# Sending exp(scores) and u through HBM to transpose them on VectorE, with q and k fetched in one DMA each

## The chip, the core and the metric

The kernel runs on one core of a Trainium2 chip. The time is device microseconds of one launch, from the first to the last instruction and what lies around them; the median of three runs is given. Engines are called PE (TensorE, matmuls), DVE (VectorE), ACT (ScalarE), POOL (GpSimd) and SP (SyncE, which here only issues DMAs). Each engine works through its own list of instructions in order; semaphores make one wait for another.

## The reference

Attention within chunks of 64 tokens, 8 heads of 64 channels, feeds a low-rank mixer along the sequence and a two-layer channel network. Cut to what matters:

```python
# q, k, v: [B=8, H=8, S=576, D=64]
scores = scale * q_c @ k_c.T                    # per chunk of 64 tokens: 64x64
attn = exp(scores - scores.max()) ; attn /= attn.sum()
x = (attn @ v_c) -> [B, S, H*D = 512]
u = x + ((x^T @ U) @ V)^T                       # along the sequence, rank 32
out = u + relu(u @ w_ch1) @ w_ch2               # 512 -> 2048 -> 512
```

## The kernel before

Two batches make a *pair*: 1152 tokens, 9 tiles t of 128 tokens, 3 groups g of 3 tiles. Four pairs are worked off one after the other. fp32 products are formed from a high and a low part rounded to TensorE's fp32r type (three products for one), so u is held as uth and utl, the hidden layer as hh and hl.

The main work is 4 x 3 x 16 = 192 *blocks*: a block is one piece f of 128 hidden channels for one group. It has 12 h matmuls (L690, `hidden`), then hh by ACT (L698, relu) and hl by DVE (L703), then 9 o matmuls (L716, `project_out`). The o matmuls of block f stand behind the h matmuls of block f+1 on PE, so hh and hl have the length of 12 h matmuls and no more. All weights stay in SBUF once loaded in pair 0.

The side work of each tile has to be finished before its group's blocks, and is spread between the blocks of earlier ones:

- *Attention.* `load_qk` and `load_v` fetch q, k, v (qn, kn, vn). qT and kT: transposes. sc: 16 small matmuls (L482). mx and ex on DVE (L496, L500), exp on ACT (L504). Four PE transposes ps_eT (L452) and an ACT copy (L474) make eT. av: 16 small matmuls (L513), then row sums and the scaling on DVE (L525 to L532), which gives x.
- *Mixer.* `project_ops`: xh (ACT, L593), xl (DVE, L597), y matmuls over tiles (L604, L605). `mix_ops`: u matmul (L644), x + u on DVE (L650, written over x), four PE transposes ut (L656), then uth (ACT, L664) and utl (DVE, L669).

For q and k of all tiles but the first nine, DVE's 32x32 stream transpose (L460) is used, which turns each 32x32 square in place. A whole transpose needs the squares to be exchanged as well, and that is done by the layout of the load: the *halvings* (L382) copy q and k within HBM into buffers halfq and halfk in pieces of 32 channels (128 bytes), and L409 then fetches each tile by 8 DMAs of 64 KB, 32 partitions each, whose slowest loop runs over the 32 rows.

The order has two sources. Pair 0 is planned: each operation is an `Op` with its engine, a cost and buffers to take, and a list scheduler orders them together with the weight loads (table `WORK`) and the blocks (`STRETCHES`). `HALVES_FROM = 4` says from which block on halvings may go. From pair 0's last group on, the code is written in program order: `plan` gives a list of steps for each group (`attend`, `mixes`, `proj`), spread evenly over the 64 slots of the group (one slot ahead of each tile of a block), and each engine takes its instructions in this order where the data allow it. All later DMAs go on SP's one queue. Side work's buffers are 8 shared slots of 256 KB (`slot`); x has 10 buffers.

Of the kernel before, what the change touches and what calls it, by code (L numbers as in the profile page):

```python
# [21 lines left out]
def kernel(  # L22
# [11 lines left out]
    nc = tc.nc  # L34
# [87 lines left out]
    ROOM = {"bank": 8, "w": NF, "slot": NS, "x": NX, "y": 2, "ut": 2, "h": 2, "mx": 2, "sm": 2}  # L122
# [198 lines left out]
    def w_ops(f, after=None):  # L321
# [15 lines left out]
        for z in range(n):  # L337
            cols = slice(z * size, (z + 1) * size)

            def room(z=z):  # L340
                return wslot((size,), U32, f"wroom_{f}") if n == 1 else slot(U32, f"wroom_{f}_{z}")
# [13 lines left out]
            tag = "w" if n == 1 else "slot"  # L355
# [14 lines left out]

    loaded = {}
# [6 lines left out]
    hidden_last = [None]  # L378

    def halve(b, z, g):  # L380
        d = halves[b, z, g] = dram.tile([S, H * SQ], F32, name=f"half{'qk'[z]}_{b}_{g}")
        moved = nc.sync.dma_start(  # L382
            d.rearrange("s (h i) -> s h i", h=H),
            (q, k)[z][b, :, :, g * SQ : (g + 1) * SQ].rearrange("h s i -> s h i"),
        )
        sync = mybir.DependencyInfo(mybir.DependencyClass.Sync, mybir.DependencyReason.DATA)
        tc.add_manual_dep(moved.ins, hidden_last[0].ins.name, sync, reason="after this block")

    def halvings(pr):
        return [lambda b=b, z=z, g=g: halve(b, z, g) for b in (2 * pr, 2 * pr + 1) for z in range(2) for g in range(2)]  # L390

    def load_qk(pr, t):
# [5 lines left out]
        else:  # L398
            qn = slot(F32, "qn_" + n, (P, P // SQ, P))
            kn = slot(F32, "kn_" + n, (P, P // SQ, P))  # L400
            vn = slot(F32, "vn_" + n, (P, 2, HP, D1))
        nc.gpsimd.memset(vn[:, :, :, D:], 1.0)  # L402
        if not early(pr, t):
            for z, dst in enumerate((qn, kn)):
                for r, m, b, s0 in segments(pr, t):
                    for e in range(2):
                        for g in range(2):
                            x0 = (2 * e + g) * SQ
                            nc.sync.dma_start(  # L409
                                dst[x0 : x0 + SQ, r // SQ : (r + m) // SQ, :],  # L410
                                halves[b, z, g][s0 : s0 + m, e * P : (e + 1) * P].rearrange(
                                    "(a j) c -> j a c", j=SQ
                                ),
                            )
            loaded[pr, t] = qn, kn, vn
            return
# [5 lines left out]
    def heads(pr, t, e):  # L422
        return slice(e, None, 2) if early(pr, t) else slice(e * HP, (e + 1) * HP)
# [19 lines left out]

    def attention_ops(pr, t, *after):
        n = f"{pr}_{t}"
        st = {}
        mine = early(pr, t)

# [9 lines left out]
        def squares(z, name):  # L458
            dst = slot(F32, name + n, (P, HP, P))
            nc.vector.transpose(  # L460
                dst.rearrange("p h (a j) -> p h a j", j=SQ),
                loaded[pr, t][z].rearrange("p a (h i) -> p h a i", i=SQ),
            )
# [34 lines left out]
        def subtract(e):  # L498
            mx = st["mx"][:, e, :]
            nc.vector.tensor_sub(st["ex"][:, :, e, :], st["sc"][e], mx.unsqueeze(2).broadcast_to([P, HP, C]))  # L500

        def exp():
            exf = st["ex"].rearrange("p a b k -> p (a b k)")
            nc.scalar.activation(exf, exf, AF.Exp, scale=SCALE)  # L504

# [22 lines left out]
        def scaled(e):  # L528
# [428 lines left out]
```

## Time and profile before

| | |
|---|---|
| median of 3 runs | 988.29 us (985.99 to 989.6) |
| the profiled execution | 984.5 us |
| its span, first to last instruction | 982.7 us |
| mean granted TensorE clock | 0.99 |

The profile is of one execution. A row of a group has the instruction, its count after x, then the busy time in us and the mean ns of one, and then how long the engine stood idle just before them and which engine or DMA ended that. Rows of windows have, after the bounds and length, the busy us of PE, PEld (weight loads), DVE, ACT and POOL with instruction counts, the granted clock, the DMA engines' mean busy share and GB/s. Rows of a timeline have the start, the length, the engine and the instruction, and in brackets the idle time before it. Rows of DMAs have the queue, the count, the KB of each and the median us from issue to landing.

### The profile page before, as it was taken

The page shows a single profiled execution, that of the slowest core. Times are in us where ns is not written, and L with a number is a line of the kernel's source. Part 1 is how long each engine was busy: PE and PEld are TensorE (multiplying, and loading weights), DVE is VectorE, ACT ScalarE, POOL GpSimd, SP SyncE. Part 2 cuts the span into 40 slices and gives each one's busy share as a digit, 9 for nine tenths or more (in the row PEclk, how much of TensorE's full clock was granted, in tenths as well). Part 3 has the DMA queues.
Part 4 walks back from the last instruction along what each step waited for, and adds up shares of the span by engine and source line. Part 5 has one row for each costly group of instructions (what it writes and reads, how often), then busy time and mean ns, then how long its engine had stood idle before and what let it go on. Part 6 is the DMA issues. An engine that isn't in the chain of part 4 may idle for free.

```text
span 982.7 us, 16528 instructions
## 1 busy us (share of the span) xinstructions
PE 961.3 (98%) x6854; PEld 835.0 (85%) x6857; DVE 439.5 (45%) x867; ACT 227.5 (23%) x406; POOL 33.7 (3%) x89
## 2 busy tenths in 40 slices
PE   7899899999999999999999999999999999999998
PEld 4569799988888889888888888888888889999997
DVE  5789789874442534233443343333433333211211
ACT  4543333321321211111211221111212121111110
POOL 6500000000000000000000000000000000000000
PEclk8999999999999999999999999999999999999999
DMA  9945964146753121433332111111121000000000
GB/s 218 224 140 97 210 187 139 36 133 112 129 107 89 31 41 52 81 61 86 68 79 62 28 33 37 42 37 48 42 57 33 33 1 1 33 1 1 33 1 33
DMA packets 208123, 70.58 MB, mean 72 GB/s; under 512 B 164768, under 2 KB 200640, under 8 KB 208048
## 3 DMA queue, kind: packets, MB, share of 16 engines
q1 hardware_dynamic: 206528, 66.35, 29.9%
q0 software_dynamic: 1520, 3.17, 1.6%
q8 instruction: 54, 0.88, 0.4%
q14 instruction: 21, 0.17, 0.1%
HBM read 59.98 MB, written 23.67 MB: 85 GB/s over the span
## 4 chain that ended last, share of the span: by engine, by line
PE 91%; DMA 3%; DVE 3%; ACT 1%; SPq 1%; issue 1%; POOL 0%; DVEq 0%; ACTq 0%; POOLq 0%
PE h L690 41%; PE o L716 40%; PE sc L482 2%; PE av L513 2%; PE ut L656 2%; PE ps_eT L452 1%; DMA wraw<-in_moe_w_ch_dram 1%; PE u L644 1%; DMA qkv<-in_k_dram 1%; PE y L604 1%; PE y L605 1%; DMA uraw<-in_moe_U_dram 1%; DMA qkv<-in_v_dram 1%; PE y L611 1%; ACT qkT L474 0%
## 5 line engine op out<-in xcount | busy, mean ns | idle before, releaser
L690 PE MATMUL h<-uth,w 128*128 128x384 f32 x1536 | 424.8, 341 | 0.0
L716 PE MATMUL o<-w,hh 128*128 128x512 f32 x1152 | 359.2, 401 | 3.7 <-ACT hh L698 3.5
L690 PEld LDWEIGHTS h<-uth,w 128*128 128x128 f32 x1536 | 282.1, 188 | 8.2 <-issue 0.2
L703 DVE SCALAR_TENSOR_TENSOR hl<-h,hh 128x384 fp32r<-128x384 f32 x192 | 106.5, 555 | 361.3 <-ACT hh L698 361.1
L690 PE MATMUL h<-utl,w 128*128 128x384 f32 x768 | 260.0, 339 | 0.0
L716 PEld LDWEIGHTS o<-w,hh 128*128 128x128 f32 x1152 | 211.6, 189 | 42.2 <-ACT hh L698 5.6
L716 PE MATMUL o<-w,hl 128*128 128x512 f32 x576 | 217.7, 397 | 0.0
L698 ACT ACTIVATE hh<-h 128x384 fp32r<-128x384 f32 x192 | 94.2, 491 | 499.9 <-PE h L690 499.6
L690 PEld LDWEIGHTS h<-utl,w 128*128 128x128 f32 x768 | 144.8, 189 | 6.1 <-DVE utl L669 0.3
L716 PEld LDWEIGHTS o<-w,hl 128*128 128x128 f32 x576 | 108.7, 189 | 25.8 <-DVE hl L703 0.3
L504 ACT ACTIVATE ex<-ex 128x512 f32<-128x512 f32 x36 | 22.8, 633 | 97.0 <-DVE ex L500 94.0
L496 DVE TENSOR_REDUCE mx<-sc 128x4 f32<-128x256 f32 x72 | 27.9, 417 | 27.5 <-PE sc L482 27.4
L650 DVE TENSOR_TENSOR x<-u,x 128x512 f32<-128x512 f32 x36 | 24.3, 684 | 27.6 <-PE u L644 27.4
L460 DVE STREAM_TRANSPOSE qT<-qn 128x512 f32<-128x512 f32 x27 | 19.1, 708 | 31.8 <-PE y L604 15.6
L669 DVE TENSOR_TENSOR utl<-ut,uth 128x512 fp32r<-128x512 f32 x36 | 24.4, 687 | 19.8 <-ACT uth L664 19.8
L474 ACT COPY eT<-ps_eT 128x512 f32<-128x512 f32 x36 | 21.0, 587 | 42.6 <-PE ps_eT L452 19.8
L597 DVE TENSOR_TENSOR xl<-x,xh 128x512 fp32r<-128x512 f32 x30 | 20.5, 687 | 21.6 <-ACT xh L593 18.4
L500 DVE TENSOR_TENSOR ex<-sc,mx 128x256 f32<-128x256 f32 x72 | 28.0, 416 | 1.2 <-DVE mx L496 0.5
L664 ACT CAST uth<-ut 128x512 fp32r<-128x512 f32 x36 | 20.9, 587 | 32.2 <-PE ut L656 32.1
L532 DVE TENSOR_TENSOR x<-av,sm 128x256 f32<-128x256 f32 x72 | 27.1, 417 | 1.1
L402 POOL MEMSET vn<- 128x8 f32 x27 | 3.0, 112 | 685.1 <-PE y L605 205.3
L728 DVE TENSOR_TENSOR x<-o,x 128x512 f32<-128x512 f32 x36 | 23.1, 684 | 4.9 <-PE o L716 4.8
(84 smaller groups left out, 552.3 us busy)
## 6 DMA issues: line engine op xcount, KB each, us to landing
wraw<-in_moe_w_ch_dram SPq DMA_DIRECT2D x32, 512.0 KB, 7.1
out_dram<-x SPq DMA_DIRECT2D x36, 256.0 KB, 2.2
halfq<-in_q_dram SPq DMA_DIRECT2D x12, 576.0 KB, 6.3
halfk<-in_k_dram SPq DMA_DIRECT2D x12, 576.0 KB, 6.1
vn<-in_v_dram SPq DMA_DIRECT2D x108, 64.0 KB, 2.4
qn<-halfq SPq DMA_DIRECT2D x96, 64.0 KB, 2.0
kn<-halfk SPq DMA_DIRECT2D x96, 64.0 KB, 2.0
qkv<-in_v_dram POOLq DMA_DIRECT2D x36, 64.0 KB, 6.3
```

The lines of the kernel that those rows point to most:

```text
L474: nc.scalar.copy(dst.rearrange("p a b -> p (a b)"), st[name])
L496: nc.vector.reduce_max(mx, st["sc"][e], axis=AX.X)
L500: nc.vector.tensor_sub(st["ex"][:, :, e, :], st["sc"][e], mx.unsqueeze(2).broadcast_to([P, HP, C]))
L504: nc.scalar.activation(exf, exf, AF.Exp, scale=SCALE)
L532: nc.vector.tensor_mul(by_head[:, heads(pr, t, e), :], st["av"][e][:, :, 0:D], st["sm"][:, e].unsqueeze(2).broadcast_to([P, HP, D]),)
L650: nc.vector.tensor_add(x, st["u"], x)
L669: nc.vector.tensor_sub(ul[:, :, js], st["t"].rearrange("p (c t) -> p c t", c=NCC), uh[:, :, js])
L690: hidden_last[0] = nc.tensor.matmul(ps[:, :GN], lhsT=w[:, z, cc], rhs=u[:, cc, :], start=(n == 0), stop=(n == 3 * NCC - 1))
L698: nc.scalar.activation(hh, ps[:, :GN], AF.Relu)
L703: nc.vector.scalar_tensor_tensor(hl, ps[:, :GN], 0.0, hh, op0=ALU.max, op1=ALU.subtract)
L716: nc.tensor.matmul(acc[g, j], lhsT=h[:, js], rhs=w2[f][:, z], start=(first and i == 0), stop=(final and i == 2),)
L728: nc.vector.tensor_add(x, ps, x)
```

## The change

1. From pair 1 on (for e all but pair 1's tiles 0 and 1), e = exp(scores) and u are written to HBM (`put`): e by one DMA of 256 KB (rows esd), u by four DMAs of 64 KB in pieces of 32 channels (usd). One DMA brings each back (`fetch`, tiles es and us), in the layout that DVE's 32x32 transposes need, and DVE makes eT (L533) and uT (L703). PE loses ps_eT and ut there, ACT the copies of eT.
2. q and k of a tile come by one such `fetch` each instead of 8 DMAs. Pair 1's tiles 0 and 1 (`plain`) load q and k directly and have them transposed on PE.
3. Halvings are 48 of 288 KB instead of 24 of 576 KB, in pairs after every second block from block 13 on (`HALVES_FROM`), and later wherever the word `h` stands in a list.
4. The planned steps become fixed lists of words for each group (`FIRST`, `LATER`): t loads' transposes, s scores, q the transpose of e, l/f/u the three parts of the mixer, p projections, `.` nothing. av with its sums stands just before the next tile's softmax, in the same step as its scores.
5. The 8 shared slots become slots by kind (`SLOTS`): 3 for q and k, 2 for v, 1 each for e, eT, us and uT; xh uses the uT slot and xl the us slot. x has 9 buffers.

The core of the diff:

```diff
-    NX = 10
-    NS = 8
+    NX = 9
+    SLOTS = {"qk": 3, "e": 1, "eT": 1, "vn": 2, "us": 1, "uT": 1}
...
+    def plain(pr, t):
+        return pr == 0 or (pr == 1 and t < len(GATES))
...
+    def fetch(kept, dst):
+        nc.sync.dma_start(dst, kept.rearrange("(j a) (z c) -> z (j a) c", a=P // SQ, z=P // SQ))
+        return dst
...
-        if not early(pr, t):
+        if not plain(pr, t):
             for z, dst in enumerate((qn, kn)):
-                for r, m, b, s0 in segments(pr, t):
-                    for e in range(2):
-                        for g in range(2):
-                            x0 = (2 * e + g) * SQ
-                            nc.sync.dma_start(
-                                dst[x0 : x0 + SQ, r // SQ : (r + m) // SQ, :],
-                                halves[b, z, g][s0 : s0 + m, e * P : (e + 1) * P].rearrange(
-                                    "(a j) c -> j a c", j=SQ
-                                ),
-                            )
+                fetch(halves[pr, z][t * P : (t + 1) * P], dst)
...
+    def put(src, name, by_channel=False):
+        kept = dram.tile([P, DM], F32, name=name + "d")
+        for c in range(NCC if by_channel else 1):
+            if by_channel:
+                src_c, dst_c = (a.rearrange(f"p ({o} i) -> p c z i", c=NCC, i=SQ)[:, c] for a, o in ((src, "c z"), (kept, "z c")))
+            else:
+                src_c, dst_c = src, kept
+            nc.sync.dma_start(dst_c, src_c)
+        return kept
...
             nc.vector.transpose(
-                dst.rearrange("p h (a j) -> p h a j", j=SQ),
-                loaded[pr, t][z].rearrange("p a (h i) -> p h a i", i=SQ),
+                dst.rearrange("p h (j a) -> p a h j", j=SQ), loaded[pr, t][z].rearrange("p a (h i) -> p a h i", i=SQ)
             )
...
+        def spread_e():
+            kept = put(flat(), "es_" + n)
+            st["es"] = fetch(kept, slot("e", F32, "es_" + n, (P, P // SQ, P)))
+
+        def square_e():
+            st["eT_"] = slot("eT", F32, "eT_" + n, (P, HP, P))
+            nc.vector.transpose(
+                st["eT_"].rearrange("p h (j a) -> p a h j", j=SQ), st["es"].rearrange("p a (h i) -> p a h i", i=SQ)
+            )
...
+        def put_u():
+            st["kept"] = put(x_of[pr, t], "us_" + n, by_channel=True)
+
+        def fetch_u():
+            st["us"] = fetch(st["kept"], slot("us", F32, "us_" + n, (P, P // SQ, P)))
+
+        def square_u():
+            uT = st["t"] = slot("uT", F32, "uT_" + n)
+            nc.vector.transpose(
+                uT.rearrange("p (c j a) -> p a c j", c=NCC, j=SQ), st["us"].rearrange("p a (c i) -> p a c i", i=SQ)
+            )
...
+        if pr > 0:
+            pu = Op("SP", 2.0, put_u, ad, lat=2.0)
+            fe = Op("SP", 2.0, fetch_u, pu, take="us", lat=2.0)
+            tr = Op("DVE", 0.71, square_u, fe, take="uT", free="us")
...
-    HALVES_FROM = 4
+    TAIL = 8
+    HALVES_FROM = 13
...
+        done = behind.pop(0)[2] if len(behind) > 1 else []
+        i = tiles.index((pr, t))
+        return [*done, soft[0], lambda: begin_next(i), *soft[1:]]
...
+    LATER = {
+        0: "t6 q5 s6 l3 h f3 h t7 q6 s7 u3 p0 p1 h t8 h q7 s8 p2 p3 h . . q8 a8 p4 . l4 . f4 l5 . . u4 f5 . . . u5",
```

The names below end in pair, tile (or group and block) and a buffer number: hl_2_0_3 is pair 2, group 0, block 3; kn_2_7 pair 2, tile 7.

DVE, at the start of pair 2's blocks. Before:

```order
L703 SCALAR_TENSOR_TENSOR hl_2_0_1_5386<-h_2_0_1_5371,hh_2_0_1_5384 128x384
L496 TENSOR_REDUCE mx_2_7_5417<-sc0_2_7_5398 128x4
L496 TENSOR_REDUCE mx_2_7_5417<-sc1_2_7_5399 128x4
L500 TENSOR_TENSOR ex_2_7_5416<-sc0_2_7_5398,mx_2_7_5417 128x4x64
L500 TENSOR_TENSOR ex_2_7_5416<-sc1_2_7_5399,mx_2_7_5417 128x4x64
L703 SCALAR_TENSOR_TENSOR hl_2_0_2_5442<-h_2_0_2_5427,hh_2_0_2_5440 128x384
L460 STREAM_TRANSPOSE qT_2_8_5466<-qn_2_8_5336 128x512
L703 SCALAR_TENSOR_TENSOR hl_2_0_3_5486<-h_2_0_3_5471,hh_2_0_3_5484 128x384
```

After (line numbers are those of the changed kernel: L475 kT, L533 eT, L703 uT, L760 hl, L687 the addition of u, L718 utl):

```order
L785 TENSOR_TENSOR x_1_8_3550<-o_1_8_4582,x_1_8_3550 128x512
L475 STREAM_TRANSPOSE kT_2_7_5322<-kn_2_7_5231 128x4x128
L687 TENSOR_TENSOR x_2_3_4640<-u_2_3_5273,x_2_3_4640 128x512
L760 SCALAR_TENSOR_TENSOR hl_2_0_1_5271<-h_2_0_1_5256,hh_2_0_1_5269 128x384
L760 SCALAR_TENSOR_TENSOR hl_2_0_2_5311<-h_2_0_2_5296,hh_2_0_2_5309 128x384
L533 STREAM_TRANSPOSE eT_2_6_5327<-es_2_6_5249 128x4x128
L703 STREAM_TRANSPOSE uT_2_3_5416<-us_2_3_5294 128x4x128
L760 SCALAR_TENSOR_TENSOR hl_2_0_3_5344<-h_2_0_3_5329,hh_2_0_3_5342 128x384
L718 TENSOR_TENSOR utl_2_1_5419<-uT_2_3_5416,uth_2_1_5418 128x4x128
```

The transposes of e and u now stand one behind the other between hl of blocks 2 and 3, in place of one transpose of q, and the maxima and exponents' inputs of tile 7 have moved behind these rows.

SP's queue at the same place. Before (L409 q and k, L432 v):

```order
L409 DMA qn_2_8_5336<-halfq_5_0_2528 32x4x128
L409 DMA qn_2_8_5336<-halfq_5_1_2797 32x4x128
L409 DMA kn_2_8_5337<-halfk_5_0_2876 32x4x128
L409 DMA kn_2_8_5337<-halfk_5_1_3195 32x4x128
L409 DMA kn_2_8_5337<-halfk_5_0_2876 32x4x128
L409 DMA kn_2_8_5337<-halfk_5_1_3195 32x4x128
L432 DMA vn_2_8_5338<-in_v_dram 64x4x64 x3
L382 DMA halfk_7_1_5352<-in_k_dram 4608x1x32
L731 DMA out_0_dram<-x_1_6_3040 128x512
L731 DMA out_0_dram<-x_1_7_3388 128x512
```

After (L400 every fetch, L454 the puts, L389 halvings, L435 v, L788 the output):

```order
L435 DMA vn_2_7_5232<-in_v_dram 64x4x64 x2
L400 DMA kn_2_7_5231<-halfk_2_2641 128x4x128
L435 DMA vn_2_7_5232<-in_v_dram 64x4x64 x2
L788 DMA out_0_dram<-x_1_8_3550 128x512
L454 DMA es_2_6d_5247<-ex_2_6_5240 128x512
L389 DMA halfk_3_4867<-in_k_dram 576x4x32
L454 DMA us_2_3d_5276<-x_2_3_4640 512x1x32 x3
L400 DMA es_2_6_5249<-es_2_6d_5247 128x4x128
L454 DMA us_2_3d_5276<-x_2_3_4640 512x1x32
L400 DMA qn_2_8_5389<-halfq_2_2375 128x4x128
L400 DMA us_2_3_5294<-us_2_3d_5276 128x4x128
L389 DMA halfq_3_4548<-in_q_dram 576x4x32
```

Eight DMAs of q and k (qn_2_8 has two more ahead of these rows) became one each, and between them stand now the puts and fetches of e and u, the output rows and the halvings.

SP's queue in the loading part of pair 0 (wraw: the weights as they come, two DMAs each). Before:

```order
L326 DMA wraw_5_1093<-in_moe_w_ch1_dram 128x4x256
L330 DMA wraw_5_1093<-in_moe_w_ch2_dram 128x1024
L382 DMA halfq_2_0_1120<-in_q_dram 4608x1x32
L382 DMA halfq_2_1_1162<-in_q_dram 4608x1x32
L326 DMA wraw_6_1166<-in_moe_w_ch1_dram 128x4x256
L330 DMA wraw_6_1166<-in_moe_w_ch2_dram 128x1024
L382 DMA halfk_2_0_1190<-in_k_dram 4608x1x32
L382 DMA halfk_2_1_1232<-in_k_dram 4608x1x32
L326 DMA wraw_7_1236<-in_moe_w_ch1_dram 128x4x256
L330 DMA wraw_7_1236<-in_moe_w_ch2_dram 128x1024
```

After:

```order
L327 DMA wraw_5_1090<-in_moe_w_ch1_dram 128x4x256
L331 DMA wraw_5_1090<-in_moe_w_ch2_dram 128x1024
L327 DMA wraw_6_1153<-in_moe_w_ch1_dram 128x4x256
L331 DMA wraw_6_1153<-in_moe_w_ch2_dram 128x1024
L327 DMA wraw_7_1219<-in_moe_w_ch1_dram 128x4x256
L331 DMA wraw_7_1219<-in_moe_w_ch2_dram 128x1024
L327 DMA wraw_8_1278<-in_moe_w_ch1_dram 128x4x256
L331 DMA wraw_8_1278<-in_moe_w_ch2_dram 128x1024
L327 DMA wraw_9_1357<-in_moe_w_ch1_dram 128x4x256
L331 DMA wraw_9_1357<-in_moe_w_ch2_dram 128x1024
L389 DMA halfq_1_1400<-in_q_dram 576x4x32 x2
L327 DMA wraw_10_1414<-in_moe_w_ch1_dram 128x4x256
```

The halvings of q and k of batches 2 and 3 (before) no longer stand between weights 5, 6, 7 and 8; the first ones (now of pair 1's buffer) stand behind weight 9.

More of the change, by code (lines that the diff above doesn't have):

```diff
@@ L618, in project_ops @@
                 continue
-            h = Op("ACT", 0.62, high, xs[i + 4 * e], take="slot")
-            lo = Op("DVE", 0.69, low, h, take="slot")
-            prev = Op("PE", 0.47, product, lo, prev, u_done, take="" if i else "bank", free="slot slot")
+            h = Op("ACT", 0.62, high, xs[i + 4 * e], take="uT")
+            lo = Op("DVE", 0.69, low, h, take="us")
+            prev = Op("PE", 0.47, product, lo, prev, u_done, take="" if i else "bank", free="uT us")
             steps.append([h, lo, prev])
@@ L818 @@
                 last = prev
-            if blocks >= HALVES_FROM and second:
+            if blocks >= HALVES_FROM and blocks % 2 == 1 and second:
                 rank[0] = 0
-                in_halves = Op("SP", 0.6, second.pop(0), prev[0], lat=6.0)
+                for _ in range(2):
+                    Op("SP", 0.6, second.pop(0), prev[0], lat=3.0)
             if blocks in gates:
-                assert not second
                 rank[0] = 0
-                attention_ops(1, gates[blocks], prev[0], in_halves)
+                attention_ops(1, gates[blocks], prev[0])
     assert blocks == 2 * NF
@@ L848 @@
     manual.__exit__(None, None, None)
-    to_halve = {}
+    assert not second
+    to_halve = [w for b in range(4, B) for w in halvings(b)]
     tiles = [(pr, t) for pr in range(NPAIR) for t in range(NT)]
@@ L860, in flush @@
                 finish(pr, g, f, j, ps)
-    def step(*group):
-        return lambda: [o.run() for o in group]
-    def attend(ts):
-        steps = []
-        prev = None
-        for key in ts:
-            i = tiles.index(key)
-            _, q, k, sc, et, av = attention_ops(*key)
-            def ahead(i=i):
-                if i + 1 < len(tiles) and tiles[i + 1] not in loaded:
-                    load(*tiles[i + 1])
-                pr, t = tiles[i]
-                if pr + 1 < NPAIR:
-                    todo = to_halve.setdefault(pr + 1, halvings(pr + 1))
-                    for _ in range(-(-len(todo) // max(1, NT - 1 - t))):
-                        todo.pop(0)()
-            steps += [ahead, step(*q)] + ([prev[0]] if prev else [])
-            steps += [step(*k)] + ([prev[1]] if prev else []) + [step(*sc)]
-            prev = step(*et), step(*av)
-        return steps + (list(prev) if prev else [])
@@ L886, in mixes, with begin_next @@
-    def mixes(pr, ts):
-        steps = []
-        st = [[step(*z) for z in mix_ops(pr, t, None, [None, None])] for t in ts]
-        for i in range(len(st) + 1):
-            steps += ([st[i][0]] if i < len(st) else []) + ([st[i - 1][1]] if i else [])
-        return steps
-    def proj(pr, e):
-        return [step(*z) for z in project_ops(pr, e, [None] * NT)[0]]
+    behind = []
+    def begin_next(i):
+        if i + 1 < len(tiles) and tiles[i + 1] not in loaded:
+            load(*tiles[i + 1])
@@ new lines, in attend @@
+    def attend(pr, t, what):
+        if what == "turn":
+            _, q, k, soft, square, av = attention_ops(pr, t)
+            behind.append((soft, square, av))
+            return [*q, *k]
+        if what == "square":
+            return behind[0][1]
+        if what == "last":
+            return behind.pop(0)[2]
+        soft = behind[-1][0]
+        done = behind.pop(0)[2] if len(behind) > 1 else []
+        i = tiles.index((pr, t))
+        return [*done, soft[0], lambda: begin_next(i), *soft[1:]]
@@ new lines, with go @@
+    mixing = {}
+    def go(pr, g, word):
+        if word == ".":
+            return
+        if word == "h":
+            if to_halve:
+                to_halve.pop(0)()
+            return
+        kind, i = word[0], int(word[1:])
+        if kind in "tsqa":
+            at = pr + 1 if g else pr
+            if at < NPAIR:
+                do(attend(at, i, {"t": "turn", "s": "scores", "q": "square", "a": "last"}[kind]))
+            return
+        at = pr + 1 if g == 2 else pr
+        if at == NPAIR:
+            return
+        if kind == "p":
+            e = int(g == 0)
+            if i == 0:
+                mixing["p"] = project_ops(at, e, [None] * NT)[0]
+            do(mixing["p"][i])
+        elif kind == "l":
+            mixing[i] = mix_ops(at, i, None, [None, None])
+            do(mixing[i][0])
+        else:
+            do(mixing[i]["lfu".index(kind)])
@@ L917 @@
                 slots += 1
-                while done < len(steps) and done * (NF * 4 - 6) < len(steps) * slots:
-                    steps[done]()
+                while done < len(steps) and done * (NF * 4 - TAIL) < len(steps) * slots:
+                    go(pr, g, steps[done])
                     done += 1
```

130 lines of the change are left out of this document (76 added, 54 removed), and 2 rows, old and new, of the table LATER.

## The prediction

> **What bounds the kernel now.** I read the page's head and busy times first, then the chain that ended last, then three windows.
>
> ```profile
> span 982.7 us, 16528 instructions
> PE 961.3 (98%) x6854; PEld 835.0 (85%) x6857; DVE 439.5 (45%) x867; ACT 227.5 (23%) x406; POOL 33.7 (3%) x89
> PE 91%; DMA 3%; DVE 3%; ACT 1%; SPq 1%; issue 1%; POOL 0%; DVEq 0%; ACTq 0%; POOLq 0%
> PE h L690 41%; PE o L716 40%; PE sc L482 2%; PE av L513 2%; PE ut L656 2%; PE ps_eT L452 1%; DMA wraw<-in_moe_w_ch_dram 1%; PE u L644 1%; DMA qkv<-in_k_dram 1%; PE y L604 1%; PE y L605 1%; DMA uraw<-in_moe_U_dram 1%; DMA qkv<-in_v_dram 1%; PE y L611 1%; ACT qkT L474 0%
> 72.57 4.18 PE o L716 x18
> ...
> 100.00:125.00 25.00, 21.46 (x95) 18.17 (x94) 19.38 (x24) 7.05 (x9) 0.00 (x0) 0.90 1.20 208
> 500.00:525.00 25.00, 25.00 (x217) 21.85 (x217) 11.52 (x28) 5.38 (x10) 0.23 (x2) 1.00 0.13 33
> 900.00:925.00 25.00, 25.00 (x127) 22.68 (x126) 5.23 (x9) 2.95 (x6) 0.00 (x0) 1.00 0.09 32
> ```
>
> TensorE (PE) is 91% of the chain, h and o products 81. The windows (PE, PEld, DVE, ACT, POOL busy, then granted clock and DMA share) say when: from pair 1 on PE never rests, at clock 1.00; only in the loading stretch does it stand (21.46 of 25). So a PE instruction taken out later is worth its time, and any wait newly put before PE costs its full length. The first full run of o products starts at 72.57, so a tile takes (982.7 − 72.6)/36 = 25.3 us, and a block of 12 h and 9 o products 4.2.
>
> **Gain: PE transposes.** 25 of e and 27 of u (four matmuls each) go, and q and k of two tiles come back onto PE: 25 + 27 − 4 = 48 fewer.
>
> ```profile
> L452 PE MATMUL ps_eT<-ident,ex 128*128 128x128 f32 x144 | 23.5, 282 | 1.5 <-ACT ex L504 1.5
> L656 PE MATMUL ut<-ident,x 128*128 128x128 f32 x144 | 21.8, 274 | 0.7 <-DVE x L650 0.6
> 893.18 0.60 PE L656 MATMUL ut<-ident,x 128*128 128x128 f32 x4
> 893.54 0.71 PE L716 MATMUL o<-w,hh 128*128 128x512 f32 x2
> 894.09 0.39 PE L716 MATMUL o<-w,hl 128*128 128x512 f32 x1
> ...
> 895.01 0.64 PE L716 MATMUL o<-w,hh 128*128 128x512 f32 x2
> 895.48 0.40 PE L716 MATMUL o<-w,hl 128*128 128x512 f32 x1
> ...
> 558.53 0.66 PE L452 MATMUL ps_eT<-ident,ex 128*128 128x128 f32 x4
> 559.16 1.66 PE L716 MATMUL o<-w,hh 128*128 128x512 f32 x6
> ```
>
> The timeline prices one: from its start to the next product 893.18 → 893.54 is 0.36 us, and the pair behind it takes 0.55 instead of 0.47 (895.01 → 895.48), so 0.44. That gives 48 × 0.44 = 21 us. Bounds: 0.36 × 48 = 17; by 558.53 → 559.16 (0.63, a wait included) 30.
>
> **Gain: loading stretch.** The halvings (copies of q and k into HBM in 128-byte pieces) no longer stand between the loads of weights 6 to 9 on SP.
>
> ```profile
> 116.74 0.40 PE L716 MATMUL o<-w,hl 128*128 128x512 f32 x1
> 119.11 1.12 ACT L87 ACTIVATE wroom<-wraw 128x1024 f32<-128x1024 f32 x1 [5.50 <-DMA wraw<-in_moe_w_ch_dram]
> 120.13 0.48 ACT L698 ACTIVATE hh<-h 128x384 fp32r<-128x384 f32 x1
> 120.66 1.22 PE L716 MATMUL o<-w,hh 128*128 128x512 f32 x2 [3.52 <-ACT hh L698]
> 121.68 0.63 PE L716 MATMUL o<-w,hl 128*128 128x512 f32 x1
> 122.11 1.05 PE L716 MATMUL o<-w,hh 128*128 128x512 f32 x2
> halfq<-in_q_dram SPq DMA_DIRECT2D x12, 576.0 KB, 6.3
> ```
>
> ACT waited 5.50 us for a weight; hh, which PE needed, was queued behind that wait; PE stood 3.52, and afterwards issued o products 0.42 apart (121.68 → 122.11) where 0.23 is usual (895.48 less 895.01, halved). So an idle stretch of this length costs PE about 3 more. I take 6.5 us for this gain, between 0 (another late weight takes its place) and 8. The row also shows the mechanism that I fear below: one late DMA, an in-order engine, PE idle.
>
> **Loss: e and u now go out to HBM and back.** Nothing in before does this; it is bounded by neighbouring rows.
>
> ```profile
> out_dram<-x SPq DMA_DIRECT2D x36, 256.0 KB, 2.2
> vn<-in_v_dram SPq DMA_DIRECT2D x108, 64.0 KB, 2.4
> qn<-halfq SPq DMA_DIRECT2D x96, 64.0 KB, 2.0
> ...
> q1 hardware_dynamic: 1280, 0.53, 19.1%
> ...
> 656.23 4.64 SPq L409 DMA_DIRECT2D qn<-halfq  x8
> 664.67 1.92 SPq L432 DMA_DIRECT2D vn<-in_v_dram  x3
> ```
>
> The window 656 to 666 holds 1024 pieces of 512 bytes and 256 of the 1280 packets that are small: 19.1% of 16 engines × 10 us is 30.6 us, so at most 0.030 us a piece, and I take 0.028. A fetch of 256 KB is 512 pieces, 14.4 us of engine time: 0.9 us spread over 16 engines, 3.6 over 4. With the 1.8 us left of the 2.0-us qn row after its 128 pieces on 16 engines, it lands 2.7 or 5.4 us after issue. Which holds decides the case. Every spread and fetch of before steps through 32 rows or more in its slowest loop; the new fetch reads its source as 4 outer steps of 64 KB (z) around 128 rows. If engines are dealt pieces, 16 work; if they are dealt outer steps, 4. No row of before has so short an outer loop. I take 5.4: the nearest thing is one 64-KB step on one engine, 128 × 0.028 + 1.8 = 5.4.
> The Trainium skill, page "DMA: Bandwidth & Descriptors", section "Rules for kernel authors", states that a slowest dimension of size under 16 confines the DMA to at most that many engines. By it the landing is 5.4 us and the sum the forecast's; without it the sum is that of the first rival. No run here shows it yet.
>
> Putting e is one DMA of the out_dram kind, 2.2 us. Putting u is four, 0.64 apart (1.92 for three), the last landing about 4.2 us after the first issue.
>
> ```profile
> L460 DVE STREAM_TRANSPOSE qT<-qn 128x512 f32<-128x512 f32 x27 | 19.1, 708 | 31.8 <-PE y L604 15.6 <-PE ps_eT L452 9.4 <-DMA vn<-in_v_dram 4.0
> L703 DVE SCALAR_TENSOR_TENSOR hl<-h,hh 128x384 fp32r<-128x384 f32 x192 | 106.5, 555 | 361.3 <-ACT hh L698 361.1
> L500 DVE TENSOR_TENSOR ex<-sc,mx 128x256 f32<-128x256 f32 x72 | 28.0, 416 | 1.2 <-DVE mx L496 0.5
> L504 ACT ACTIVATE ex<-ex 128x512 f32<-128x512 f32 x36 | 22.8, 633 | 97.0 <-DVE ex L500 94.0 <-DMA vn<-in_v_dram 3.0
> L650 DVE TENSOR_TENSOR x<-u,x 128x512 f32<-128x512 f32 x36 | 24.3, 684 | 27.6 <-PE u L644 27.4
> L644 PE MATMUL u<-ys,vst 128*128 128x512 f32 x40 | 15.6, 415 | 0.2 <-DVE ex L500 0.2
> L664 ACT CAST uth<-ut 128x512 fp32r<-128x512 f32 x36 | 20.9, 587 | 32.2 <-PE ut L656 32.1
> ```
>
> From e's scores to eT: 4 × 0.416 + 0.63 + 2.2 + 2.7 + 0.70 = 7.9 us, or 10.6. The order gives it about three blocks (12.6), so alone it is hidden. From u's product to uT: 0.42 + 0.68 + 4.2 + 2.7 + 0.71 = 8.7, or 11.4. On DVE uT stands straight before hl of block 3, which can run 8.9 us after u (9 o, 12 h, 9 o and 12 h products at 2.1 us a set, and hh's 0.48); the o products that read it come some 1.5 later (2.1 of the next block's h and 0.46 of its first two o, less 0.48 for hh and 0.56 for hl). So u is just on time at 2.7 and about 1 us late at 5.4, even with nothing queued. Behind a late uT wait hl (then PE), uth on ACT, and the next tile's work.
>
> The queue makes it worse. At the place shown in the order, SP issues four fetches (k, e, q, u) and u's puts within some 10 us. On 4 engines that is 4 × 3.6 = 14.4 us; the puts are 2048 pieces at (6.3 − 1.8) × 16/4608 = 0.0156 us, 2.0 on each of 16; 16.4 in 10 leaves 6.4 us queued. The whole period books the four engines for 14.4 + 2.0 + halvings 24 × 4.5/27 = 4.0 + out and e 0.9 each and v about 1 = 23 of 25.3 us, so the queue hardly drains. I take PE 5 us late per tile, between 2 (most of it overlaps the 1.5 us slack, or falls where nothing waits) and 8 (1 + 6.4, rounded up): 27 × 5 = 135. Six or seven of these should be long enough to slow the clock as above, 3 us each: 20.
>
> Small parts, one answer each. DVE gains 48 transposes, 48 × 0.70 = 34 us, on an engine busy 440 of 983 that idles 361.3/192 = 1.9 us before each hl: 0 by itself. They now write every fourth element; no row shows that, and at twice the time it is 34 more, still off the path. ACT loses 21 net copies of the uth row's size, 0.587 each: 0, since ACT is busy 227 of 983 and the uth row's idle time ends on PE, not the other way round. q and k by one DMA instead of eight: SP's issue 4.64 us (the qn row ×8) becomes one issue; the landing, 4.64 × 7/8 + 1.8 = 5.9 before against 5.4, is hidden either way, but cover is gone when the engines are booked, as above. Moving av and sums next to scores changes no work: it can save or cost one short wait of PE per tile (av and sc hold 2% of the chain each), bounds 3 either way, and I take 0. Halvings move the same bytes: 0. The slots by tag (one for e, one for us) make a fetch wait for its predecessor's reader, which stands earlier on DVE anyway: 0.
>
> Sum, from the profiled execution's 984.5 us (982.7 span): 984.5 − 21 − 6.5 + 135 + 20 = 1112; the median of the runs, 988.29, stands 3.8 above it: 1116, said as 1115. Own range: 2 us a tile and no clock loss, 984.5 + 3.8 − 27.5 + 54 = 1015; 8 us and 27 for the clock, 960.8 + 216 + 27 = 1204.
>
> **The rivals.** First, faster: the fetch uses all 16 engines and lands in 2.7 us. For it: DMA share is only 0.13 at 500 to 525. Then e's and u's chains fit (7.9 in 12.6, 8.7 in 8.9), leaving waits of 0 to 12 us over 27 tiles, 4 taken: 988.3 − 27.5 + 4 = 965, from 958 to 973. It turns at 1 us of PE wait per tile: 27 × 1 eats the 27.5.
> Second, that price exactly: the fetch is short, but DVE's fixed order makes it wait about 1 us per tile at uT, since only 0.2 us is spare there. That gives about 988, no change. Against it: PE has 1.5 us of slack behind hl.
> Third, the fetch takes four engines, yet queues do not build, as SP waits for semaphores between issues and thins them out: 1 us per tile, net about 988 to 1000.
> That the PE transposes are removed but their time stays cannot be, as PE was never idle there.
>
> **Chances.** Four engines with queues 0.63; sixteen engines 0.27; the two cases between 0.10, of which 0.05 within 0.5% (a difference below that is about what this measurement cannot tell from no change), 0.02 faster, 0.03 slower. From the first case 0.62 slower and 0.01 same. Together: faster 0.29, same 0.06, slower 0.65. The first case's own range is 1015 to 1204. The overall range takes in the fast rival's lower end and the slow case's bound, 958 to 1204, since the queue's price is bounded no better than that; about 0.15 is left outside.
>
> **What would show it.** Right: fetch rows (es, us, qn, kn) landing at 5 us or more; DVE idle before eT, uT and kT put down to DMA; PE idle before o products put down to hl or to xh; granted clock below 1.00 in later windows. Also expected: e and u PE transposes down to 44 and 36 matmuls, and no 5.50 us ACT wait on wraw near 119. Wrong: fetches landing under 3 us with the clock at 1.00 in pairs 1 to 3; then the time is near 965.

## The result, and the profile after

The change made the kernel slower: 1226.0 us median against 988.8 (four executions of each, one more than in the table above), ratio 1.240 (95% interval 1.236 to 1.244). All times from here on are medians over executions in the chip's usual, faster state; one execution of the run at 993.0 us below took 1552.6 us at a clock of 0.557 and does not count. The direction was forecast, and so was the kind of mechanism: slow fetches, a late DVE, an idle PE, a lower clock. But the time is above the stated range (1204), with nearly twice the loss. The page's head, busy times and chain, and the same three windows as before:

```profile
span 1225.7 us, 16155 instructions
PE 1014.8 (83%) x6663; PEld 866.7 (71%) x6663; DVE 501.0 (41%) x915; ACT 212.1 (17%) x385; POOL 34.0 (3%) x89
DMA 40%; PE 39%; DVE 9%; SPq 6%; issue 3%; ACT 2%; POOL 1%; DVEq 0%; POOLq 0%; ACTq 0%
...
100.00:125.00 25.00, 25.00 (x126) 22.59 (x126) 24.38 (x29) 9.74 (x14) 0.00 (x0) 1.00 0.26 65
500.00:525.00 25.00, 20.64 (x149) 17.60 (x148) 9.73 (x19) 3.52 (x7) 0.11 (x1) 0.93 0.47 101
900.00:925.00 25.00, 18.10 (x132) 14.90 (x131) 9.03 (x19) 3.20 (x6) 0.11 (x1) 0.86 0.24 68
```

PE's share of the chain fell from 91% to 39% and DMA's rose from 3% to 40%. The loading stretch is better than before (25.00 busy of 25, clock 1.00); the two later ones are worse. PE stood idle 1225.7 − 1014.8 = 211 us where it was 21. It was also busy 53.5 us longer, though 48 groups of transposes are gone: the mean granted clock (the share of full speed that TensorE was allowed) is 0.908 where it was 0.990. The trace's clock record stands at one half for 227 us in 36 stretches, against 22 us in 4 before.

The groups of waiting transposes, and what is left of e's and u's on PE. The last figures in a row are DVE's idle time before them and what ended it:

```profile
L475 DVE STREAM_TRANSPOSE qT<-qn 128x512 f32<-128x512 f32 x25 | 27.3, 1091 | 2.9 <-PE o L773 2.9
L475 DVE STREAM_TRANSPOSE kT<-kn 128x512 f32<-128x512 f32 x25 | 27.3, 1094 | 83.9 <-DMA kn<-halfk 83.9
L533 DVE STREAM_TRANSPOSE eT<-es 128x512 f32<-128x512 f32 x25 | 27.1, 1084 | 179.5 <-DMA es<-es_4d 26.8 <-DMA es<-es_3d 24.1 <-DMA es<-es_6d 23.3
L703 DVE STREAM_TRANSPOSE uT<-us 128x512 f32<-128x512 f32 x27 | 29.5, 1092 | 145.7 <-DMA us<-us_2d 23.2 <-DMA us<-us_0d 19.3 <-DMA us<-us_7d 18.7
L467 PE MATMUL ps_eT<-ident,ex 128*128 128x128 f32 x44 | 7.6, 305 | 3.5 <-ACT ex L525 3.5
L693 PE MATMUL ut<-ident,x 128*128 128x128 f32 x36 | 5.3, 276 | 0.1
```

DVE waits three times per tile, at kT, eT and uT, together 83.9 + 179.5 + 145.7 = 409 us. Before, e and u had no transposes on DVE, and kT's row was:

```profile
L460 DVE STREAM_TRANSPOSE kT<-kn 128x512 f32<-128x512 f32 x27 | 18.6, 689 | 1.3 <-DMA vn<-in_v_dram 0.3
```

PE's longest waits in the changed kernel (us in total, times, longest):

```profile
PE av L544 <- DVE eT L533: 63.9, 13, 8.1
PE o L773 <- DVE hl L760: 42.5, 22, 5.7
PE o L773 <- ACT hh L755: 36.9, 19, 5.0
PE y L641 <- ACT xh L630: 19.4, 3, 7.7
```

The first is the wait for e: av, the product of e and v, waits for eT.

What a late uT looks like stands in the chain, at the place of the order that was shown (tiles 2_6 to 2_8). Columns are start, length and what it was:

```profile
666.35 5.86 DMA kn<-halfk
...
672.30 1.09 DVE kT L475
...
673.91 0.47 DVE hl L760
...
676.58 6.15 DMA us_3d<-x
...
682.80 6.42 DMA us<-us_3d
...
689.25 1.10 DVE uT L703
...
692.41 0.80 PE y L641
```

Of these 26 us three transfers, one behind the other, fill 18.4. The two fetches take 5.9 and 6.4 us, where 5.4 was forecast for one with nothing queued. But a *put* (us_3d, the last of its four DMAs of 64 KB) takes 6.15 too, where the forecast had 2.3 (4.2 from the first issue, less 1.92 for the three issues). It is the longest of the 27; their median is 3.2.

e's way at the same place, from the timeline:

```profile
670.05 0.35 SPq L454 DMA_DIRECT2D es_6d<-ex  x1
673.24 0.67 DVE L687 TENSOR_TENSOR x<-u,x 128x512 f32<-128x512 f32 x1
673.94 1.93 SPq L454 DMA_DIRECT2D us_3d<-x  x3
675.96 0.57 SPq L400 DMA_DIRECT2D es<-es_6d  x1
682.41 1.08 DVE L533 STREAM_TRANSPOSE eT<-es 128x512 f32<-128x512 f32 x1 [7.58 <-DMA es<-es_6d]
```

e is put at 670.05. The put lands at 673.98 (the last update of its semaphore in the trace), 3.9 us after issue, behind k's fetch. e's fetch goes at 675.96 only: in SP's order it stands behind three of u's puts, these waited for DVE's addition at 673.24, and that stood behind kT, which had waited for k's fetch until 672.30. So from e's put to eT 12.4 us pass, where the forecast had 2.2 + 5.4 = 7.6.

Read from the semaphores in the same way, this place is typical for e and a long one for u (15.3 us from the first put to the landing of the fetch). The median from e's put to the landing of its fetch is 12.6 us (the put 4.1, the fetch 8.1), and from the issue of u's first put also 12.6 (the four puts 6.3, the fetch 5.9), where the forecast had 7.6 and 4.2 + 5.4 = 9.6.

### The profile page after: what moved, and what is told of

It reads as the page before. It is cut to its first block, busy times and chain, and to the rows that moved or that the text cites. A ratio compares the mean times of both kernels' runs of the same rounds, so it can differ in the third digit from the quotient of the medians.

```text
span 1225.7 us, 16155 instructions
## 1 busy us (share of the span) xinstructions
PE 1014.8 (83%) x6663; PEld 866.7 (71%) x6663; DVE 501.0 (41%) x915; ACT 212.1 (17%) x385; POOL 34.0 (3%) x89
## 4 chain that ended last, share of the span: by engine, by line
DMA 40%; PE 39%; DVE 9%; SPq 6%; issue 3%; ACT 2%; POOL 1%; DVEq 0%; POOLq 0%; ACTq 0%
PE o L773 19%; PE h L746 16%; DMA kn<-halfk 8%; SPq L454 2%; DMA es<-es_5d 2%; DMA es<-es_4d 2%; SPq L435 2%; DMA es<-es_3d 2%; PE av L544 2%; DMA es<-es_8d 2%; DVE uT L703 2%; DVE eT L533 2%; DMA us<-us_3d 2%; DVE kT L475 2%; DMA us<-us_2d 1%
## 5 line engine op out<-in xcount | busy, mean ns | idle before, releaser
L773 PE MATMUL o<-w,hh 128*128 128x512 f32 x1152 | 378.4, 421 | 36.9 <-ACT hh L755 36.9
L773 PE MATMUL o<-w,hl 128*128 128x512 f32 x576 | 234.6, 429 | 42.8 <-DVE hl L760 42.5
L760 DVE SCALAR_TENSOR_TENSOR hl<-h,hh 128x384 fp32r<-128x384 f32 x192 | 103.6, 550 | 188.7 <-ACT hh L755 188.6
L533 DVE STREAM_TRANSPOSE eT<-es 128x512 f32<-128x512 f32 x25 | 27.1, 1084 | 179.5 <-DMA es<-es_4d 26.8
L544 PE MATMUL av<-vn,eT 64*64 64x65 f32 x864 | 29.5, 272 | 75.0 <-DVE eT L533 63.9
L703 DVE STREAM_TRANSPOSE uT<-us 128x512 f32<-128x512 f32 x27 | 29.5, 1092 | 145.7 <-DMA us<-us_2d 23.2
L544 PEld LDWEIGHTS av<-vn,eT 64*64 64x64 f32 x864 | 23.9, 177 | 89.5 <-issue 89.5
L475 DVE STREAM_TRANSPOSE kT<-kn 128x512 f32<-128x512 f32 x25 | 27.3, 1094 | 83.9 <-DMA kn<-halfk 83.9
L713 ACT CAST uth<-uT 128x512 fp32r<-128x512 f32 x27 | 16.7, 619 | 253.5 <-DVE uT L703 253.5
L630 ACT CAST xh<-x 128x512 fp32r<-128x512 f32 x30 | 18.5, 618 | 123.9 <-DVE x L563 117.6
L687 DVE TENSOR_TENSOR x<-u,x 128x512 f32<-128x512 f32 x36 | 24.2, 684 | 30.8 <-PE u L681 30.6
L496 PE MATMUL sc<-kT,qT 64*64 64x64 f32 x864 | 25.6, 254 | 4.5 <-DVE hl L760 4.4
```

Source lines behind the costliest of these rows:

```text
L475: nc.vector.transpose(dst.rearrange("p h (j a) -> p a h j", j=SQ), loaded[pr, t][z].rearrange("p a (h i) -> p a h i", i=SQ))
L496: nc.tensor.matmul(ps[e][cs, hp * C : (hp + 1) * C], lhsT=st["qT_"][rows, hp, cs], rhs=st["kT_"][rows, hp, cs], start=True, stop=True,)
L533: nc.vector.transpose(st["eT_"].rearrange("p h (j a) -> p a h j", j=SQ), st["es"].rearrange("p a (h i) -> p a h i", i=SQ))
L544: nc.tensor.matmul(ps[e][cs, hp * D1 : (hp + 1) * D1], lhsT=st["eT_"][rows, hp, cs], rhs=vn[rows, c, hp, :], start=True, stop=True,)
L703: nc.vector.transpose(uT.rearrange("p (c j a) -> p a c j", c=NCC, j=SQ), st["us"].rearrange("p a (c i) -> p a c i", i=SQ))
L760: nc.vector.scalar_tensor_tensor(hl, ps[:, :GN], 0.0, hh, op0=ALU.max, op1=ALU.subtract)
```

## The experiments

All are edits of the changed kernel unless something else is said; times are to be compared with 987 to 989 for the kernel before, which was timed again beside each set of runs.

**Four DMAs for one.** Each fetch is cut at its outer loop:

```diff
-        nc.sync.dma_start(dst, kept.rearrange("(j a) (z c) -> z (j a) c", a=P // SQ, z=P // SQ))
+        rows = kept.rearrange("(j a) (z c) -> z j a c", a=P // SQ, z=P // SQ)
+        for z in range(P // SQ):
+            nc.sync.dma_start(dst[z * SQ : (z + 1) * SQ], rows[z])
```

> Every fetch (q, k, e, u) is issued as 4 DMAs, one for each outer step z, instead of one DMA with an outer loop of 4; bytes, pieces, layout and order stay. Theory A (one such DMA is worked off by 4 engines, so it lands 5.4 us after issue and the four engines queue): the waits of eT, uT and kT for DMAs fall from 179.5, 145.7 and 83.9 us to under 60 together, clock 0.98 or more, time 965 to 1010. Rival B (16 engines were at work; what costs is SP's in-order queue and the round trip through HBM): SP now issues 306 DMAs more, so the time stays at 1226 or rises, 1200 to 1300.

Measured 1073.0 us, ratio 1.087 (1.084 to 1.091), clock 0.964. The same bytes and pieces, with 306 DMAs more to issue, are 153 us faster. So the outer loop of 4 costs that much net of the added issues, and rival B falls. Theory A's number falls too: 1073 is not 965 to 1010. DVE's waits at kT, eT and uT went from 409 us to 45 + 121 + 112 = 278, not under 60.

**The disputed cost by itself.** A kernel that only moves 256 KB at a time, every fetch ended by a DVE transpose; one execution, six repetitions of each kind.

> Computes nothing of the reference: transfers of 256 KB alone, one after the other, six times each, every one ended by a DVE transpose that waits for it. Theory A: the fetch in one DMA (f_one) lands about 5.4 us after issue, four DMAs by outer step (f_split) about 3.4 after the first issue, one DMA from a buffer in which every partition's 2 KB lie together (f_zmaj) 2.5; two fetches at once (f_twin) end 3.6 us apart, of four (f_quad) the last lands about 16 us after the first issue. Rival B: f_one 2.7, f_twin 0.9 apart, f_quad about 5.5. Both: a DVE transpose with every fourth element written 1.09 us, with contiguous output 0.70.

The timeline, one repetition of each kind; each DVE row starts when the fetch above it has landed (f_pad's row takes in the next repetition's issue as well):

```profile
14.05 0.54 SPq L101 DMA_DIRECT2D f_one<-rowmaj  x1
19.33 1.08 DVE L83 STREAM_TRANSPOSE last<-f_one 128x512 f32<-128x512 f32 x1 [7.31 <-DMA f_one<-rowmaj]
...
58.59 0.71 DVE L87 STREAM_TRANSPOSE last<-f_split 128x512 f32<-128x512 f32 x1 [4.40 <-DMA f_split<-rowmaj]
...
143.70 0.33 SPq L116 DMA_DIRECT2D f_zmaj<-zmaj  x1
146.47 0.71 DVE L87 STREAM_TRANSPOSE last<-f_zmaj 128x512 f32<-128x512 f32 x1 [5.15 <-DMA f_zmaj<-zmaj]
...
256.48 6.69 SPq L129 DMA_DIRECT2D f_pad<-padded  x2
261.93 0.71 DVE L87 STREAM_TRANSPOSE last<-f_pad 128x512 f32<-128x512 f32 x1 [5.47 <-DMA f_pad<-padded]
```

The one-DMA fetch lands in 19.33 − 14.05 = 5.3 us, the one with an outer loop of 128 and 2 KB pieces in 2.8, and DVE idled 4.4 until the four DMAs, issued one after the other, had landed (3.4 was forecast). f_pad, for which no number was forecast, decides between piece size and loop: it has the 2 KB pieces of f_zmaj, but an outer loop of 4 (a gap in the buffer keeps the steps apart), and takes 261.93 − 256.48 = 5.5. So it is the loop and not the size of the pieces. The fetches meant to run two and four at once ran as a stream, so their single landings can't be read; the stream's rate can:

```profile
330.00:395.00 65.00, 25.18 (x24) 0.00 (x0) 1.00 0.28 86
```

With nothing but such fetches under way the 16 engines are 0.28 busy, 4.5 of them, at 86 GB/s (packet times can overlap, so this is no exact count). At 86 GB/s a fetch of 256 KB takes 3.0 us of the stream, where the prediction booked 3.6. The trace's semaphore records count more sharply: each f_one and f_pad gets 5 updates, each DMA of f_two (see the last section) 3, each f_zmaj and each of the four of f_split 16. That fits one update for each of 4, 2 or 16 engines, and one more where not all 16 take part. In the changed kernel every fetch of q, k, e and u has 5, every put 16. The Trainium skill, page "DMA: Bandwidth & Descriptors", section "Rules for kernel authors", has a loop of 4 outermost confine a DMA to at most 4 engines; the trace agrees, 5.3 and 5.5 us against 2.8.

**u back on PE.** In the mixer's steps (a second line keeps the transposes' place in the lists):

```diff
-        if pr > 0:
+        if pr > 9:
             pu = Op("SP", 2.0, put_u, ad, lat=2.0)
```

> u of pairs 1 to 3 is transposed on PE again (27 x 4 transposes back, about +12 us of PE), without its puts and fetches; e, q and k as in the change. Theory A: the four engines lose a quarter of their fetches and DVE the uT wait: 1050 to 1110. Rival C (e's round trip alone sets the time, u hides behind it): 1180 to 1240.

Measured 1172.0 us, ratio 1.186 (1.184 to 1.189): 54 us less, and neither theory's number. DVE now idles 203.7 us before eT and 96.3 before kT. With q and k, e's round trip keeps most of the loss, so it is not hidden as the forecast had it.

**One DMA with an outer loop of 128.** e and u lie in HBM so that the outer loop of their fetch is the 128 partitions (their puts write that layout), and q and k come by 4 DMAs:

```diff
-        kept = dram.tile([P, DM], F32, name=name + "d")
+        kept = dram.tile([P // SQ, P, P], F32, name=name + "d")
...
+        nc.sync.dma_start(dst.rearrange("p a c -> p (a c)"), kept.rearrange("z (j a) c -> (z j) (a c)", a=P // SQ))
```

> e and u are kept in HBM so that each partition's 2 KB lie together, and one DMA with an outer loop of 128 fetches each; q and k by 4 DMAs each. Theory A: landing of the e and u fetches 2.5 us, time 960 to 985, below the kernel before. Rival B: 1150 or more, since the round trips, their order on SP and the DVE order are all still there.

Measured 1018.9 us, ratio 1.032 (1.029 to 1.035). Of the 237 us lost 207 are back. By the first run 153 of them come with the short outer loops alone; the other 54 come with fetching e and u by one DMA in 2 KB pieces instead of four in 512-byte pieces, and with the puts' new layout (alone, 2.8 us to the landing instead of 4.4). Yet it is still slower than before, and theory A's 960 to 985 is missed by 34. The same round trip of u in its chain:

```profile
532.62 1.96 DMA us_2d<-x
...
534.66 2.71 DMA us<-us_2d
...
537.46 1.13 DVE uT L710
```

The put lands in 1.96 us here and in 6.15 in the changed kernel. Over all tiles the median round trips are 6.3 us for e and 7.3 for u, where both were 12.6. The DVE groups of this run show what the round trips still cost:

```profile
L710 DVE STREAM_TRANSPOSE uT<-us 128x512 f32<-128x512 f32 x27 | 29.6, 1097 | 67.6 <-DMA us<-us_3d 12.5 <-DMA us<-us_2d 11.4 <-DMA us<-us_7d 9.6
L482 DVE STREAM_TRANSPOSE kT<-kn 128x512 f32<-128x512 f32 x25 | 27.5, 1101 | 49.0 <-DMA kn<-halfk 49.0
L540 DVE STREAM_TRANSPOSE eT<-es 128x512 f32<-128x512 f32 x25 | 27.4, 1094 | 81.7 <-DMA es<-es_3d 13.4 <-DMA es<-es_2d 12.5 <-DMA es<-es_8d 11.8
```

**A put behind a fetch, by itself.** Whether the puts are late because of the fetches was then measured apart, again in one execution.

> Computes nothing of the reference: a put of 256 KB (one DMA as for e, then four DMAs in 128-byte pieces as for u) and its reading back, six times each, alone (none), right behind one fetch with an outer loop of 4 (one), behind one fetch of the same bytes with an outer loop of 128 (zmaj), behind two of the first kind (double). Measured: from the issue of the put's last DMA to the issue of the read that waits for its landing. Theory J (a put has pieces on all engines, so it lands only when the four engines that the fetch keeps busy for 3.6 us are through with it): e 2.0 alone, 2.0 to 3 behind zmaj, about 5.5 behind one and 9 behind double. Rival K (the late puts of the changed kernel have another cause, such as the halvings or SP): 2 to 3 us in all four.

The timeline of SP, one repetition of e's put (kept) each: alone, behind one fetch with an outer loop of 4, behind one with 128, behind two with 4. The row after each put is the read that waits for its landing:

```profile
10.12 0.36 SPq L125 DMA_DIRECT2D kept<-src  x1
12.42 0.33 SPq L127 DMA_DIRECT2D back_none_e<-kept  x1
...
83.10 1.34 SPq L125 DMA_DIRECT2D kept<-src  x1
88.94 0.33 SPq L127 DMA_DIRECT2D back_one_e<-kept  x1
...
200.62 0.43 SPq L125 DMA_DIRECT2D kept<-src  x1
204.08 0.32 SPq L127 DMA_DIRECT2D back_zmaj_e<-kept  x1
...
297.67 3.04 SPq L125 DMA_DIRECT2D kept<-src  x1
304.64 0.34 SPq L127 DMA_DIRECT2D back_double_e<-kept  x1
```

From issue to landing 2.3, 5.8, 3.5 and 7.0 us (over the repetitions 5.4 to 5.8, 3.2 to 3.5 and 6.7 to 7.0 behind a fetch). Rival K falls: a put that follows a fetch with an outer loop of 4 is held by it, 3.5 us longer than alone, and 1.2 longer behind the same bytes with an outer loop of 128. Theory J holds in kind; its numbers were 2 to 3 behind zmaj, where 3.5 was measured, and 9 behind two, where it is 7.0 from the put's issue and 9.1 from that of the first fetch. u's four puts behave alike: from the first issue to the read 3.5 us alone, 6.2 to 6.6 behind one, 3.9 to 4.3 behind zmaj, 7.6 to 8.2 behind two. SP's issue of e's put lengthens as well, from 0.36 to 1.34 and 3.04.

**e and u both on PE, then q and k by 4 DMAs.** The edits of the runs above, joined.

> e and u of all tiles are transposed on PE; the rest is the change (q and k by one fetch each, word lists, slots by kind, halvings from block 13). PE gets 52 x 4 transposes back, about +23 us. Theory A (a fetch of 4 outer steps is slow wherever it stands): kT still waits for kn, so still slower than before, 1010 to 1090. Rival D (only the round trips of e and u cost, q and k by one DMA are hidden): 985 to 1005.

Measured 1025.4 us, ratio 1.038 (1.036 to 1.041): theory A's range. That is 147 us less than with u alone on PE, so e is by far the dearer of the two.

> As the run with e and u on PE, and q and k by 4 DMAs each. Theory A: what is left of the change is the loading stretch and the lists, 975 to 995. Rival E (the word lists, the slots by kind and the later loads of q, k and v cost by themselves, whatever the engines do): 1000 to 1040, with kT still waiting for kn.

Measured 998.0, ratio 1.011 (1.008 to 1.014), between the two theories. So fetching q and k by one DMA costs 27 us and is not hidden, and 998 is still above before. The waits at kT (total us, times, longest) of the two runs, the first with one fetch, the second with four DMAs:

```profile
DVE kT L476 <- DMA kn<-halfk: 92.9, 25, 6.2
```

```profile
DVE kT L478 <- DMA kn<-halfk: 55.2, 24, 3.7
```

**Other queues.** To the run with 1018.9 us, v on POOL's queue (`queue = nc.gpsimd` in `load_v`), then the halvings too.

> As the run with e and u in one piece of 2 KB per partition and q and k by 4 DMAs (1019 us), but v of all tiles is fetched from POOL's queue, not SP's: SP issues 108 DMAs fewer, and its waits for a v slot (v <- av) no longer stand ahead of k's fetch. Theory F (the rest of the loss is SP's queue, where a DMA that waits holds those behind it): 975 to 1000. Rival G (the rest is the length of the round trips themselves and DVE's order): 1012 to 1025.

Measured 1006.3, ratio 1.019 (1.015 to 1.023): between F and G.

> As the last, and the halvings too are issued from POOL's queue, which wait for a block's end before they go. Theory F: 5 to 20 us below the last run, 960 to 990. Rival G: no difference from the last run within 5 us, or slower, as the copies in 128-byte pieces now come at other times.

Measured 1012.5, ratio 1.026 (1.024 to 1.027). So v's place on SP's queue costs 13 of the 1018.9, and moving the halvings gains nothing (6 us slower, as rival G had it). Theory F's numbers are missed both times.

> e and u on PE, q and k by 4 DMAs each, and v of all tiles from POOL's queue. Theory F (SP's queue: a v that waits for its slot holds k's fetch, and DVE waits at kT with hl behind it): 980 to 990, kT's wait of 55 us at least halved. Rival E (the word lists and the slots by kind themselves): 996 to 1002.

Measured 993.0, ratio 1.005 (1.003 to 1.007). kT's wait fell from 55.2 to 42.0 us, not to half: between F and E.

**One round trip at a time**, on 16 engines.

> q and k by 4 DMAs each; e through HBM with 2 KB pieces and one DMA on 16 engines; u on PE. Between 998 us (both on PE) and 1019 us (both through HBM in this layout). Theory H (u's round trip, four puts and a wait on SP for their landing, is the longer and holds SP): near 998, 990 to 1003. Rival I (e's, whose eT stands first in DVE's order): near 1019, 1010 to 1022.

> The other half: u through HBM with 2 KB pieces and one DMA on 16 engines, e on PE, q and k by 4 DMAs each. Theory H: near 1019, 1008 to 1022. Rival I: near 998, 990 to 1003.

Measured 1008.7, ratio 1.022 (1.020 to 1.025), for e alone and 1004.2, ratio 1.017 (1.014 to 1.019), for u alone, against 998.0 for neither and 1018.9 for both. Neither H nor I: each round trip costs by itself, 11 and 6 us net, though each takes PE transposes away. The 6 is hardly more than the spread of single executions, 6 to 7 us in each of these runs.

**The halvings alone, in the kernel before.**

```diff
-    HALVES_FROM = 4
+    HALVES_FROM = 13
```

> The kernel before with one number changed: halvings from block 13 on, not from block 4, so that they no longer stand between the loads of weights 5 to 9. The prediction's term: the 3.5 us idle of PE near 117 and the half clock behind it go, 6.5 us less, 980 to 983. Rival: another late transfer (a halving that pair 1's first fetches wait for) takes the place, 985 to 992.

Measured 982.5 us, ratio 0.995 (0.993 to 0.997): 5 us faster, inside the forecast, and the one version here that beats both kernels. Its window of the loading stretch shows why; before, PE was busy 21.46 there at clock 0.90:

```profile
100.00:125.00 25.00, 25.00 (x126) 22.65 (x126) 23.66 (x29) 9.23 (x12) 0.00 (x0) 1.00 0.12 43
```

## Why the prediction was right and wrong

*The choice of four engines* was right in its price: 5.3 us alone against 5.4 forecast, and 153 of the 237 us go when only the outer loop goes.

*PE transposes.* They went as counted (44 and 36 matmuls are left). Their 21 us was not measured by itself.

*The loading stretch* was right: 5 us of the 6.5 forecast, shown alone. In its window PE's idle 3.5 us and the half clock are gone; ACT still waits 5.5 us for a weight in that run, but near 156 us, where PE hardly idles (24.8 busy of 25).

*The price per tile, and of the clock, is the step that failed*: "I take PE 5 us late per tile", counted at uT alone, and 20 us for the clock. By the two traces, PE's added idle time is 211 − 21 = 190 us; PE's added busy time is 53.5, plus the 21 of transposes that are gone, so some 75 for issue at a lower granted clock. That is 190 in place of 135 and 75 in place of 20. The idle time is 7.0 us a tile, still inside the forecast's bound of 8; the clock is far outside its bound of 27, and it is what took the time past 1204. Its record bears the 75 out: PE was busy at half clock for 157 us where it was 14, and half of the difference, the time lost if half the clock does half the work, is 72. "Six or seven" idle stretches were to bring the clock down, at 3 us each; the record has 32 stretches more than before, at 2.2 each. What made the waits so much longer and more frequent:

- The puts were priced as if alone (2.2 for e; 4.2 to the last landing of u), though a queue of 6.4 us was worked out a paragraph later. A put has to land before its fetch may go, so the queue counts twice in each round trip. By itself, a put behind such a fetch takes 5.8 instead of 2.3; in the changed kernel the medians are 4.1 for e's put and 6.3 for u's four. With fetches of 8.1 and 5.9 the round trips take 12.6 us each, in place of 7.6 and 9.6.
- The lateness was counted once a tile, at uT. The trace has DVE waiting at kT, eT and uT, so hl and PE are held at up to three places, and PE's largest wait, 63.9 us, is at av for eT, which the forecast had at nothing.
- SP's order ties the places together, as e's way above shows: a late k made the addition late, that u's puts, and these e's fetch. How much of the loss this tie makes was measured only for v's place on SP, 13 us in the run at 1018.9.

Taken out one after the other, u's round trip gives back 54 us (1226.0 to 1172.0), e's 147 (to 1025.4) and the one-DMA fetch of q and k 27 (to 998.0). In another order the shares may differ.

*That e's round trip "alone … is hidden"* was wrong: with 12.6 us for put and fetch in place of 7.6, e's 10.6 us from the scores to eT become some 15.6, more than the 12.6 of the three blocks that were to cover it. eT is DVE's longest wait (179.5 us), and with an outer loop of 128 and u on PE e's round trip still costs 11 us net. That q and k are "hidden either way" was wrong as well, 27 us with nothing else on four engines; the prediction had added only that their cover is gone when the engines are booked.

*The rival at 965 was wrong too.* With fetches that land in about 3 us the time is 1019, not 965, so the forecast's waits of 0 to 12 us were far too small even with short fetches. DVE still idles 198 us before the three transposes. From 998 to 1019 is the net of what the round trips cost and of the PE transposes that they save: at the prediction's 0.44 us, 52 groups are 23 us, so by that estimate the round trips cost some 44. Whether eT and uT placed later in DVE's order would hide them was not tried.

*What was costed at nothing.* With e and u on PE, q and k by 4 DMAs and the better loading stretch, the kernel takes 998.0, while the kernel before with that loading stretch takes 982.5: 15.5 us for what is left of the change: the word lists, the slots by kind, the nine buffers of x, the new loads and halvings, two tiles of q and k on PE and the longer transposes. DVE idles 55.2 us before kT there, against 1.3. 5 go with v's place on SP; how the other ten divide was not tried. The transposes with every fourth element written take 1.09 us where they took 0.70, inside the bound of twice the time; but "off the path" was wrong, since a transpose that has been waited for stands on the chain with its whole length (uT, eT and kT are 2% of it each).

## What to carry to other kernels

Look at the outermost loop of a DMA before its bytes: a reshaped layout with 4 steps outside can cost more than the DMAs it saves, and laying the buffer out so that the loop is the 128 partitions brought the same 256 KB in 2.8 us instead of 5.3. A round trip through memory holds two landings in a row, each with the queue of its moment, so price both, and see what else stands on the issuing queue between them. An instruction taken off the bounding engine is worth its time only if what replaces it arrives before an in-order engine needs it: here eT and uT stood on DVE ahead of an hl that PE waited for. And when waits are added up, count the stretches that bring the clock down as well: here they cost 75 us beside 190 of waiting.

## What the runs showed of the hardware that was not expected

A DMA of 256 KB behind a fetch with an outer loop of 4 lands late, 5.8 us after issue instead of 2.3, and the queue that issues it is held as well: SP's issue took 0.36 alone, 1.34 behind one such fetch and 3.04 behind two. Cutting the fetch into two DMAs, each with an outer loop of 2, made it slower than one with 4. Their timeline, both issued from 84.47 on, the transpose at the landing:

```profile
84.47 2.03 SPq L111 DMA_DIRECT2D f_two<-rowmaj  x2
92.69 1.08 DVE L83 STREAM_TRANSPOSE last<-f_two 128x512 f32<-128x512 f32 x1 [8.26 <-DMA f_two<-rowmaj]
```

That is 8.2 us against 5.3, as if both had gone to the same two engines (each had the 3 semaphore updates named above); which engines they used was not seen. And a 32x32 transpose that writes every fourth element takes 1.08 us where contiguous output takes 0.71.
